# A spectral layer and a rational MoE on one core: the first block's load in two parts, the opening stage reordered

## The chip, the cores and the metric

One core of one Trainium2 chip. The metric is the device time of one execution in microseconds (us); lower is better.

## The reference, cut to what matters

```python
X = np.fft.rfft(x, axis=1)                       # x: 4 x 3008 x 256
Yr = Xr @ w_r - Xi @ w_i + b_r
Yi = Xr @ w_i + Xi @ w_r + b_i
Yr = np.sign(Yr) * np.maximum(np.abs(Yr) - 0.01, 0.0)
Yi = np.sign(Yi) * np.maximum(np.abs(Yi) - 0.01, 0.0)
y = np.fft.irfft(Y, n=3008, axis=1)
h = y.reshape(12032, 256) @ w_in                 # 256 x 2048
P = a[0] + a[1] * h + a[2] * h**2 + a[3] * h**3
Q = 1.0 + abs(b[0]) * np.abs(h) + abs(b[1]) * h**2
out = (P / (Q + 1e-6)) @ w_out                   # 2048 x 256
```

The MoE weights `w_in` and `w_out` come as 64-bit floats and are turned into two 32-bit parts (high and low) on the chip.

## The kernel before, in words

The transform of length 3008 = 47 x 64 is done in two stages of matmuls each way. Per batch element b there are 16 tasks `f1_task` (47-point stage; each copies a 96x512 tile `a` out of PSUM and stores it in HBM, `s1`), 12 tasks `f2_task` (64-point stage on tiles read back from `s1`; the result is split into a high and a low part, `x`), 24 halves `m_task` (the complex mix with `w_r`, `w_i`: 24 matmuls for a pair, then the soft threshold, `yt`) and 12 tasks `i1_task` (first inverse stage; copied as `zt` and stored in HBM, `s2`). `i2_task` does the second inverse stage for a block of five columns, on a tile `ct` loaded from `s2` by `load_c`, and splits it into `xsh` and `xsl`. Then come the MoE units: 8 for each of 26 blocks, each with `g1_mm` (12 matmuls into `h`), a chain on ScalarE, GpSimd and VectorE that starts with ScalarE's Abs (`m<-h`, L356), and `g2_mm` (12 matmuls, or 4 in the last blocks).

All instructions are placed by hand (`manual_schedule`, L485): each engine runs its queue in the order in which the Python code issues it, and every transfer of the program goes out from SyncE (SP), also in order; on that queue a transfer waits until the one eight before it has landed. The order around the change is this:

- *Opening* (L486 to L587). Seven filler matmuls (`warm`, on zeros), the loads of batch element 0, its 16 `f1` tasks with eight stores to `s1`, then loads: `f2` (L563), `wt` (L567), two parts of `b_all` read back from `s1` (256 and 512 KB, L569 and L570), `f2` again, the small inputs `sel`, `bsb`, `eye` (L573 to L580). `prepare` (L501) splits `wt` and builds `selr`, `bias` and `minus`. 28 fillers.
- *Turns* (L588 to L621), p = 0 to 14: `f2` task p, mix p-2, inverse p-3 of batch element 0. In between `convert` runs steps of the weight conversion `from_f64` (five steps to a 512 KB raw piece, 16 pieces; two ScalarE reads L465 and L466, VectorE steps, a ScalarE split L481, a VectorE subtraction): HC[p] steps ahead of the mix, HM[p] behind it, at most two pieces at once. `more_raw` loads two pieces a turn. The copies of `zt` are on VectorE (L272), and stores of `zt` wait in `late` until `flush` in the next turn.
- *Last stage* (L622 to L635): the rest of the conversions, `load_c(0)` as one transfer, eight `f1` tasks of batch element 1 (copies on ScalarE, five buffers), `i2` for block 0 in two halves.
- *The main loop* (L650 on): unit i with parts of the transform of the next batch element between its steps.

PSUM: `bank` gives the tags `ft`, `h` (two buffers each) and, while `early` holds, `acc0`/`acc1` for the mix.

```python
copy(i % 2 if b == 0 else 0, at.rearrange("p j d -> p (j d)"), pt[:96])      # L167
copy(b == 0, zt.rearrange("p k d -> p (k d)"), pt.rearrange("p k d -> p (k d)"))  # L272
```

Of the kernel before, what the change touches and what calls it, by code (L numbers as in the profile page):

```python
# [30 lines left out]
WARM = 28  # L31
HC = (0, 0, 3, 3, 3, 3, 3, 3, 3, 3, 3, 3)
HM = (0, 0, 4, 4, 4, 4, 4, 4, 4, 4, 4, 4, 4, 4)
# [62 lines left out]
def spectral_moe(ctx, tc, t, out):  # L96
# [23 lines left out]
    early = [1]  # L120
    s1 = {}
# [28 lines left out]

    a_t = {}

    def f1_task(b, i):
        c, r = divmod(i, 2)
        if i == 0:
            s1[b] = dram.tile([NK, NG, 2, NJ, D], F32, tag="s1", name="s1")
        pt = bank(b, "f1" if r else "")
        nc.tensor.matmul(out=pt[:96], lhsT=f1, rhs=xin[b, c][:, 2 * r:2 * r + 2, :].rearrange("p j d -> p (j d)"),  # L158
                         start=True, stop=True)
        yield  # L160
        if b == 0:
            if not r:
                a_t[0] = const.tile([128, 4, D], F32, tag=f"wsp{c}", name="a")[:96]
            at = a_t[0][:, 2 * r:2 * r + 2]
        else:
            at = (pro if early else sm).tile([128, 2, D], F32, tag="a", name="a", bufs=5 if early else 3)[:96]
        copy(i % 2 if b == 0 else 0, at.rearrange("p j d -> p (j d)"), pt[:96])  # L167
        yield
        if r:
            del xin[b, c]  # L170
            ahead = 4 if b == 1 and c < 4 else 2
            if b and c + ahead < NJ // 4 and not (b == 1 and c in (2, 3)):
                load_x(b, c + ahead)
        if b == 0:
            if r:
                nc.sync.dma_start(out=s1[b].rearrange("k g c j d -> (k g c) j d")[:, 4 * c:4 * c + 4, :], in_=a_t[0])
            return
        o = 4 * c + 2 * r
        nc.sync.dma_start(out=s1[b].rearrange("k g c j d -> (k g c) j d")[:, o:o + 2, :], in_=at)

    late = []

    def flush():
        while late:
            late.pop(0)()
# [77 lines left out]
    def i1_task(b, p):  # L263
        if p == 0:
            s2[b] = dram.tile([NK, NG, 2, NJ, D], F32, tag="s2", name="s2")
        yt = y_t.pop((b, p))
        pt = bank(b, "i1").rearrange("p (k d) -> p k d", k=2)
        for k in range(2):
            nc.tensor.matmul(out=pt[:, k, :], lhsT=g1[:, 2 * p + k, :], rhs=yt[:, k, :], start=True, stop=True)  # L269
        yield  # L270
        zt = sm.tile([128, 2, D], F32, tag="a", name="zt", bufs=3)
        copy(b == 0, zt.rearrange("p k d -> p (k d)"), pt.rearrange("p k d -> p (k d)"))  # L272
        yield
        dst = s2[b][2 * p:2 * p + 2].rearrange("k g c j d -> (g c j) k d")
        late.append(lambda: nc.sync.dma_start(out=dst, in_=zt))
# [3 lines left out]
    c_t = {}  # L279

# [204 lines left out]
    with tc.manual_schedule():  # L485
# [7 lines left out]
        def warm(n):  # L493
            pt = bank(1, "")
            for _ in range(n):
                nc.tensor.matmul(out=pt, lhsT=idle[:, :128], rhs=idle, start=True, stop=True)
# [4 lines left out]
        def prepare():  # L501
            for wt, h, l in zip(wts, ("wrh", "wih"), ("wrl", "wil")):
                nc.scalar.activation(out=wmix[h], in_=wt, func=ACTF.Copy)
                nc.vector.tensor_tensor(out=wmix[l], in0=wt, in1=v32(wmix[h]), op=ALU.subtract)
# [10 lines left out]

        w_in = t["w_in"].rearrange("(c p) f -> p c f", p=128)
# [5 lines left out]
        running = []  # L522

# [9 lines left out]
        def convert(n):  # L533
            while n:
                if len(running) < 2 and len(done) < len(raws) and (not running or running[0][1] >= 2):
# [4 lines left out]
                pick = running.pop(0)  # L540
                pick[1] += 1
                n -= 1
                if pick[1] < STEPS:
                    next(pick[0])
                    running.append(pick)
                else:
                    drain(pick[0])

# [20 lines left out]
        load_all(0, 2)  # L569
        load_all(2, 4)  # L570
        load_f2(4, 12)
        sel = pro.tile([4, 130], F32, tag="sel", name="sel", bufs=1)
        nc.sync.dma_start(out=sel, in_=t["sel"])  # L573
        bsb = pro.tile([4, D], F32, tag="bsb", name="bsb", bufs=1)
        blo = pro.tile([4, D], F32, tag="blo", name="blo", bufs=1)
        for k, nm in enumerate(("b_r", "b_i")):
            nc.sync.dma_start(out=bsb[2 * k:2 * k + 2, :],
                              in_=t[nm].rearrange("(o d) -> o d", o=1).to_broadcast([2, D]))
        eye = pro.tile([128, 128], F32, tag="eye", name="eye", bufs=1)
        nc.sync.dma_start(out=eye, in_=t["minus"])  # L580
        prepare()
# [51 lines left out]
        for _ in range(4):  # L633
            for g in pair:
                next(g, None)  # L635
# [121 lines left out]
```

## Time and profile before

| | |
|---|---|
| median of 3 runs | 1498.63 us (1495.12 to 1498.64) |
| profiled execution: its own time | 1499.35 us |
| its span | 1497.6 us |
| TensorE matmuls, busy | 1472.0 us, 98% of the span |
| VectorE, busy | 1390.6 us, 93% |
| ScalarE, busy | 1279.7 us, 85% |
| GpSimd, busy | 478.2 us, 32% |
| bytes read and written in HBM | 49.96 and 37.49 MB |
| first MoE matmul (`h`, L332) | 118.04 us |

Times are counted from the start of the span. A busy TensorE is not TensorE at its peak, since matmuls overlap; idle time of an engine counts only where another waits for it. "Granted clock" is the share of full speed (2.4 GHz) that the chip gave TensorE.

### The profile page before, as it was taken

How to read it: one execution, taken by the hardware profiler on the slowest of the kernel's cores; microseconds unless marked ns; L12 is line 12 of the kernel's file. 1: busy time of each engine (PE TensorE's matmuls, PEld its weight loads, DVE VectorE, ACT ScalarE, POOL GpSimd, SP SyncE). 2: the span in 40 equal slices, each digit the busy share in tenths (PEclk: the TensorE clock that was granted, in tenths of full speed). 3: DMA queues.
4: the chain of work that ended last, by engine and by line, in shares of the span. 5: the costliest groups of instructions: out<-in, count | busy, mean ns of one | idle time of the engine just before them, and what ended most of it. 6: DMA issues, size and time to landing. Idle time of an engine off the chain costs nothing.

```text
span 1497.6 us, 19703 instructions
## 1 busy us (share of the span) xinstructions
PE 1472.0 (98%) x7342; PEld 1229.0 (82%) x7343; DVE 1390.6 (93%) x1349; ACT 1279.7 (85%) x1517; POOL 478.2 (32%) x230
## 2 busy tenths in 40 slices
PE   8998999999999999999999999999999999999997
PEld 3876999999878999989878999998986777777776
DVE  2765989999999899999999999999999999999998
ACT  2657888889889889898899989898888999999986
POOL 0102222323323222332323343333333343333332
PEclk9999999999999999999999999999999999999999
DMA  8934111111132111110233011101010000000000
GB/s 265 363 96 149 46 45 42 41 55 33 61 115 76 35 42 42 41 56 29 59 106 91 28 35 48 35 27 48 21 48 14 26 14 27 26 13 27 8 14 22
DMA packets 52976, 88.72 MB, mean 59 GB/s; under 512 B 5032, under 2 KB 37104, under 8 KB 52752
## 3 DMA queue, kind: packets, MB, share of 16 engines
q1 hardware_dynamic: 52880, 87.46, 18.5%
q8 instruction: 58, 0.95, 0.3%
q14 instruction: 38, 0.31, 0.1%
HBM read 49.96 MB, written 37.49 MB: 58 GB/s over the span
## 4 chain that ended last, share of the span: by engine, by line
PE 87%; DVE 6%; issue 3%; DMA 2%; ACT 2%; SPq 0%; DVEq 0%; ACTq 0%
PE acc L424 34%; PE h L332 32%; PE pft L251 7%; PE pi L302 4%; PE pft L158 3%; PE pft L211 2%; PE pft L269 2%; PE pm L251 1%; DVE t L371 1%; DVE t L388 1%; DVE p L386 1%; PE pft L233 1%; PE pi L233 1%; DVE t L373 1%; DMA s<-a 1%
## 5 line engine op out<-in xcount | busy, mean ns | idle before, releaser
L360 POOL TENSOR_TENSOR v<-w,m 128x940 f32<-128x940 f32 (+1 forms) x208 | 456.6, 2195 | 919.4 <-DVE p L386 468.3
L332 PE MATMUL h<-xsh,win 128*128 128x470 f32 (+1 forms) x1664 | 451.0, 393 | 2.4 <-DVE t L373 2.4
L424 PE MATMUL acc<-g,wsp 128*128 128x470 f32 (+1 forms) x1908 | 433.2, 375 | 3.2 <-DVE g L391 3.2
L424 PEld LDWEIGHTS acc<-g,wsp 128*128 128x128 f32 x1908 | 357.7, 189 | 53.1 <-DVE g L391 5.5
L332 PEld LDWEIGHTS h<-xsh,win 128*128 128x128 f32 x1664 | 304.9, 190 | 63.5 <-issue 22.2
L373 DVE SCALAR_TENSOR_TENSOR t<-t,small,h 128x940 f32<-128x940 f32 (+1 forms) x208 | 244.9, 1177 | 6.1
L358 ACT ACTIVATE w<-m,small 128x940 f32<-128x940 f32 (+1 forms) x208 | 241.6, 1162 | 6.9
L371 DVE TENSOR_TENSOR t<-t,h 128x940 f32<-128x940 f32 (+1 forms) x208 | 231.2, 1111 | 12.1 <-ACT t L359 11.8
L332 PE MATMUL h<-xsl,win 128*128 128x470 f32 (+1 forms) x832 | 242.4, 372 | 0.0
L365 ACT ACTIVATE y<-v 128x940 f32<-128x940 f32 (+1 forms) x207 | 202.1, 976 | 39.5 <-DVE g L391 32.6
L359 ACT ACTIVATE t<-h,small 128x940 f32<-128x940 f32 (+1 forms) x208 | 229.8, 1105 | 0.0
L366 ACT ACTIVATE y<-y 128x940 f32<-128x940 f32 (+1 forms) x207 | 203.1, 981 | 6.6
L356 ACT ACTIVATE m<-h 128x940 f32<-128x940 f32 (+1 forms) x208 | 194.2, 934 | 12.7 <-PE h L332 9.8
L391 DVE TENSOR_TENSOR g<-t,y 128x940 fp32r<-128x940 f32 (+1 forms) x158 | 178.3, 1129 | 23.2 <-PE acc L424 22.1
L383 DVE SCALAR_TENSOR_TENSOR g<-t,small,y 128x940 fp32r<-128x940 f32 (+1 forms) x158 | 192.8, 1220 | 1.6 <-ACT y L366 1.6
L388 DVE SCALAR_TENSOR_TENSOR t<-t,small,p 128x940 f32<-128x940 f32 (+1 forms) x159 | 189.9, 1195 | 0.0
L386 DVE SCALAR_TENSOR_TENSOR p<-v,g 128x940 f32<-128x940 f32 (+1 forms) x159 | 178.7, 1124 | 0.2
L332 PEld LDWEIGHTS h<-xsl,win 128*128 128x128 f32 x832 | 155.5, 188 | 20.6
L424 PE MATMUL acc<-g,f 128*128 128x470 f32 (+1 forms) x392 | 156.7, 541 | 1.6 <-DVE g L400 1.6
L424 PEld LDWEIGHTS acc<-g,f 128*128 128x128 f32 x392 | 73.6, 189 | 59.9 <-issue 54.2
L251 PE MATMUL pft<-wrh,x 128*128 128x256 f32 x288 | 75.2, 283 | 0.0
L251 PE MATMUL pft<-wih,x 128*128 128x256 f32 x288 | 75.1, 283 | 0.0
(94 smaller groups left out, 1446.8 us busy)
## 6 DMA issues: line engine op xcount, KB each, us to landing
xin<-in_x SPq DMA_DIRECT2D x32, 384.0 KB, 4.1
s<-zt SPq DMA_DIRECT2D x48, 256.0 KB, 2.2
out_t<-ob SPq DMA_DIRECT2D x50, 235.0 KB, 2.2
ct<-s SPq DMA_DIRECT2D x22, 480.0 KB, 4.3
s<-a SPq DMA_DIRECT2D x48, 192.0 KB, 2.9
bt<-s SPq DMA_DIRECT2D x36, 256.0 KB, 2.9
raw_win<-in_w_in SPq DMA_DIRECT2D x8, 512.0 KB, 8.6
raw_wsp<-in_w_out SPq DMA_DIRECT2D x8, 512.0 KB, 8.1
```

Of the source, the lines that this page charges most:

```text
L251: nc.tensor.matmul(out=pt[:, k, :], lhsT=l, rhs=r, start=False, stop=n == len(ops) - 1, skip_group_check=True)
L332: nc.tensor.matmul(out=h[:, i, :w], lhsT=l, rhs=r, start=k == 0, stop=k == len(ops) - 1)
L356: nc.scalar.activation(out=d["m"], in_=h, func=ACTF.Abs)
L358: nc.scalar.activation(out=d["w"], in_=d["m"], func=ACTF.Identity, scale=cb[:, 1:2], bias=cb[:, 0:1])
L359: nc.scalar.activation(out=d["t"], in_=h, func=ACTF.Identity, scale=a[:, 3:4], bias=a[:, 2:3])
L360: nc.gpsimd.tensor_tensor(out=d["v"], in0=d["w"], in1=d["m"], op=ALU.mult)
L365: nc.scalar.activation(out=d["y"], in_=d["v"], func=ACTF.Square, bias=C0)
L366: nc.scalar.activation(out=d["y"], in_=d["y"], func=ACTF.Abs_reciprocal_sqrt)
L371: nc.vector.tensor_tensor(out=tt, in0=tt, in1=h, op=ALU.mult)
L373: nc.vector.scalar_tensor_tensor(out=tt, in0=tt, scalar=d["a"][:, 1:2], in1=h, op0=ALU.add, op1=ALU.mult)
L388: stt(out=tt, in0=tt, scalar=a0, in1=p, op0=ALU.add, op1=ALU.subtract)
L424: nc.tensor.matmul(out=acc[n][e][:, :w], lhsT=l[:, e * 128:(e + 1) * 128], rhs=r, start=begun[n] == 1 and k == 0, stop=begun[n] == UB and ...
```

## The change

Parts that belong together: (1) the first block's `ct` is loaded by `load_first_c` in two transfers, the rows of the first 22 frequencies as soon as their stores are out, the last 8 rows after the last store; (2) six instead of eight `f1` tasks of batch element 1 run before `i2`, with six buffers, their copies in turn on ScalarE and VectorE, their stores held in `late`; two more run between the two `i2` steps, on the `h` banks; (3) the small inputs are loaded before the first stores and prepared in the 14th `f1` task, the weights `wt` come after the first part of `b_all`, whose second load is split in two, and `f2`'s first load goes into the `f1` loop; (4) conversions: eight steps a turn (four and four), up to three pieces at once, all done in turn p = 11; (5) `zt` copies are on ScalarE but for p = 10; (6) five fillers after each of the first two `f2` tasks, and 26 instead of 28 ahead.

```diff
-WARM = 28
-HC = (0, 0, 3, 3, 3, 3, 3, 3, 3, 3, 3, 3)
-HM = (0, 0, 4, 4, 4, 4, 4, 4, 4, 4, 4, 4, 4, 4)
+WARM = 26
+FILL = 6
+HC = (0, 0, 4, 4, 4, 4, 4, 4, 4, 4, 4, 4)
+HM = (0, 0, 4, 4, 4, 4, 4, 4, 4, 4, 4, 4, 0, 0)
...
-        pt = bank(b, "f1" if r else "")
+        pt = bank(b, "f1" if r or closed else "")
...
-            at = (pro if early else sm).tile([128, 2, D], F32, tag="a", name="a", bufs=5 if early else 3)[:96]
-        copy(i % 2 if b == 0 else 0, at.rearrange("p j d -> p (j d)"), pt[:96])
+            fill = early and not closed
+            at = (pro if fill else sm).tile([128, 2, D], F32, tag="a", name="a", bufs=FILL if fill else 3)[:96]
+        copy(i % 2 if early else 0, at.rearrange("p j d -> p (j d)"), pt[:96])
...
-        nc.sync.dma_start(out=s1[b].rearrange("k g c j d -> (k g c) j d")[:, o:o + 2, :], in_=at)
+        send = lambda: nc.sync.dma_start(out=s1[b].rearrange("k g c j d -> (k g c) j d")[:, o:o + 2, :], in_=at)
+        late.append(send) if early else send()
...
-        copy(b == 0, zt.rearrange("p k d -> p (k d)"), pt.rearrange("p k d -> p (k d)"))
+        copy(b == 0 and p == NK // 2 - 2, zt.rearrange("p k d -> p (k d)"), pt.rearrange("p k d -> p (k d)"))
...
+    def load_first_c(k):
+        if not first_c:
+            first_c.append(sm.tile([96, JB, D], F32, tag="c", name="ct", bufs=1))
+        r = slice(0, 4 * k) if k < NK else slice(4 * (NK - 2), 4 * NK)
+        nc.sync.dma_start(out=first_c[0][r], in_=s2[0].rearrange("k g c j d -> (k g c) j d")[r, :JB, :])
+        c_t[0] = first_c[0]
...
         def convert(n):
             while n:
-                if len(running) < 2 and len(done) < len(raws) and (not running or running[0][1] >= 2):
+                if len(running) < 3 and len(done) < len(raws) and (not running or running[-1][1] >= 2):
                     running.append([from_f64(*raws[len(done)]), 0])
                     done.append(1)
                 if not running:
                     return
-                pick = running.pop(0)
+                turn[0] += 1
+                pick = running[turn[0] % len(running)]
...
+        load_small()
         for i in range(16):
             drain(f1_task(0, i))
-        load_f2(0, 4)
+            if i == 9:
+                load_f2(0, 4)
+            if i == 13:
+                prepare_small()
         wts = []
+        load_all(0, 2)
         for nm in ("w_r", "w_i"):
...
-        load_all(0, 2)
-        load_all(2, 4)
+        load_all(2, 2)
+        load_all(4, 2)
         load_f2(4, 12)
...
+            if p < 2:
+                warm(5, "m")
             flush()
+            if p == np_ + 2:
+                load_first_c(NK - 2)
...
         flush()
-        while running or len(done) < len(jobs):
-            convert(1)
-        load_c(0)
-        for _ in range(8):
+        assert not running and len(done) == len(jobs)
+        load_first_c(NK)
+        for _ in range(FILL):
             drain(first.pop(0)[3])
-        early.clear()
+        closed.append(1)
         pro_stack.close()
...
         pair = [i2_task(0, ec) for ec in range(2)]
-        for _ in range(4):
-            for g in pair:
-                next(g, None)
+        rest_f1 = [first.pop(0)[3] for _ in range(2)]
+        for g in pair + rest_f1 + pair + pair + pair:
+            next(g, None)
+        for g in rest_f1:
+            drain(g)
+        early.clear()
```

`load_small` and `prepare_small` hold the lines on `sel`, `bsb`, `eye` that stood after the `f1` loop and in `prepare`.

The order of instructions at three places follows; line numbers of the changed kernel are some 4 to 30 higher than those of the kernel before, and the numbers behind names tell buffers apart.

ScalarE in turn p = 4, before (`raw_win4` is the fifth raw piece, `yt` the mix's threshold, L465 and L466 the two reads, L481 the split):

```order
L216 ACTIVATE x_412<-pft_407 128x4x128
L481 ACTIVATE win2_420<-e_355 128x2x256
L257 ACTIVATE yt_450<-pm_424 128x512
L465 ACTIVATE e_454<-raw_win4_276 128x512
L466 ACTIVATE r_455<-raw_win4_276 128x512
```

and in the changed kernel:

```order
L220 ACTIVATE x_425<-pft_420 128x4x128
L478 ACTIVATE e_432<-raw_win4_287 128x512
L479 ACTIVATE r_433<-raw_win4_287 128x512
L494 ACTIVATE win2_437<-e_351 128x2x256
L494 ACTIVATE win3_440<-e_404 128x2x256
L261 ACTIVATE yt_469<-pm_443 128x512
```

The fifth raw piece is now read ahead of the third `yt`, with two splits between them.

VectorE at the end of the turns, before (L476, L468, L470, L483 are conversion steps):

```order
L147 COPY zt_942<-pft_939 128x512
L260 SCALAR_TENSOR_TENSOR yt_971<-pm_945,yt_971 128x512
L476 ISA e_887<-e_887,r_888 128x1024
L468 TENSOR_SCALAR e_935<-e_935 128x512
L483 TENSOR_TENSOR wsp6_975<-e_887,wsp6_975 128x2x256
L470 SCALAR_TENSOR_TENSOR e_935<-raw_wsp7_541,e_935 128x512
L147 COPY zt_983<-pft_980 128x512
L147 COPY zt_989<-pft_986 128x512
```

and in the changed kernel:

```order
L496 TENSOR_TENSOR wsp7_919<-e_878,wsp7_919 128x2x256
L264 SCALAR_TENSOR_TENSOR yt_957<-pm_931,yt_957 128x512
L264 SCALAR_TENSOR_TENSOR yt_992<-pm_966,yt_992 128x512
L149 COPY zt_998<-pft_995 128x512
L149 COPY a_1017<-pft_1015 96x512
```

The conversions lie ahead of the last two `yt`, one `zt` copy is left, and the copies of the `f1` tasks follow.

SyncE behind the turns in the changed kernel (`s2<-zt` are stores of the inverse, `s1<-a` those of the `f1` tasks):

```order
L279 DMA s2_414<-zt_963 128x2x256
L279 DMA s2_414<-zt_998 128x2x256
L291 DMA ct_1001<-s2_414 88x1280
L279 DMA s2_414<-zt_1006 128x2x256
L291 DMA ct_1001<-s2_414 8x1280
L144 DMA xin_1019<-in_x 96x1024
```

The first part of `ct` stands between the last two stores, the second part behind the last.

## Rows read from the trace of the kernel before

**Rows 1.** Windows: TensorE, its weight loads, VectorE, ScalarE, GpSimd; clock, DMA share, GB/s
```profile
200.00:300.00 100.00, 100.00 (x556) 90.71 (x555) 94.08 (x89) 87.94 (x104) 31.29 (x14) 1.00 0.13 41
```
**Rows 2.** Timeline of TensorE, the opening: start us, us, instruction, idle before it
```profile
22.57 6.21 PE L496 MATMUL pft<-idle 128*128 128x512 bf16 x27
30.68 1.13 PE L211 MATMUL pft<-f,b_all 128*128 128x128 f32 x8 [1.90 <-DMA b_all<-s]
33.64 3.76 PE L211 MATMUL pft<-f,b_all 128*128 128x128 f32 x16 [1.83 <-DMA b_all<-s]
37.75 0.80 PE L244 MATMUL pm<-bias,selr 128*128 128x512 f32 x1 [0.35 <-DVE bias L514]
...
43.41 0.40 PE L233 MATMUL pft<-x,minus 128*128 128x512 f32 x1
```
**Rows 3.** Windows, the opening
```profile
34.00:36.00 2.00, 2.00 (x11) 2.00 (x11) 0.49 (x2) 0.21 (x1) 0.00 (x0) 0.50 1.06 366
```
**Rows 4.** Timeline of SyncE's queue: the fifth and sixth raw piece
```profile
41.86 3.33 SPq L530 DMA_DIRECT2D raw_win<-in_w_in x2
```
**Rows 5.** DMA issues in 41.8 to 43.5 us: count, KB each, us to landing
```profile
raw_win<-in_w_in SPq DMA_DIRECT2D x2, 512.0 KB, 12.8
```
**Rows 6.** Timeline of ScalarE: conversion of the fifth raw piece
```profile
54.50 0.66 ACT L465 ACTIVATE e<-raw_win 128x512 f32<-128x512 f32 x1
...
56.86 0.63 ACT L481 ACTIVATE win<-e 128x512 fp32r<-128x512 f32 x1 [1.14 <-DVE e L476]
```
**Rows 7.** Timeline of TensorE, the turns: starts of mixes, and one stall
```profile
60.52 0.48 PE L244 MATMUL pm<-bias,selr 128*128 128x512 f32 x1
...
70.56 0.50 PE L233 MATMUL pft<-x,minus 128*128 128x512 f32 x1 [1.59 <-ACT x L216]
...
82.74 0.47 PE L244 MATMUL pm<-bias,selr 128*128 128x512 f32 x1
...
87.83 0.47 PE L244 MATMUL pm<-bias,selr 128*128 128x512 f32 x1
...
92.17 0.58 PE L244 MATMUL pm<-bias,selr 128*128 128x512 f32 x1
...
97.23 0.59 PE L244 MATMUL pm<-bias,selr 128*128 128x512 f32 x1
```
**Rows 8.** Windows, sum of 60 to 100 us in pieces of 2 us
```profile
sum 40.00, PE 37.59 PEld 35.59 DVE 32.81 ACT 27.51 POOL 5.84; mean PE 1.88 PEld 1.78 DVE 1.64 ACT 1.38 POOL 0.29
```
**Rows 9.** Timeline of VectorE: the copies of the last two inverse tiles
```profile
104.61 1.28 DVE L147 COPY zt<-pft 128x512 f32<-128x512 f32 x2
```
**Rows 10.** Timeline of TensorE, the last stage
```profile
102.09 1.13 PE L269 MATMUL pft<-yt,g 128*128 128x256 f32 x4 [0.55 <-DVE yt L260]
...
105.34 6.25 PE L158 MATMUL pft<-xin,small 96*96 96x512 f32 x14 [1.26 <-DVE zt L147]
113.35 1.32 PE L302 MATMUL pi<-small,ct 96*128 96x94 f32 x10 [1.76 <-DMA ct<-s]
115.89 2.45 PE L302 MATMUL pi<-small,ct 96*128 96x94 f32 x10 [1.21 <-ACT a L149]
118.04 2.10 PE L332 MATMUL h<-xsh,win 128*128 128x470 f32 x4
```
**Rows 11.** Chain that ended last, in the main loop: twelve MoE matmuls
```profile
160.51 2.59 PE h L332 x12
```
**Rows 12.** DMA issues in 102 to 109 us, then in the first 160 us
```profile
s<-zt SPq DMA_DIRECT2D x2, 256.0 KB, 2.2
ct<-s SPq DMA_DIRECT2D x1, 480.0 KB, 4.8
...
bt<-s SPq DMA_DIRECT2D x3, 256.0 KB, 2.8
```
**Rows 13.** Timeline of ScalarE: the first MoE Abs
```profile
122.63 0.95 ACT L356 ACTIVATE m<-h 128x940 f32<-128x940 f32 x1 [3.69 <-PE h L332]
```
**Rows 14.** Windows, the last stage
```profile
116.00:118.00 2.00, 2.00 (x10) 2.00 (x11) 0.65 (x1) 0.82 (x2) 0.00 (x0) 0.50 1.01 370
```

More of the change, by code (lines that the diff above doesn't have):

```diff
@@ L120, in spectral_moe @@
     early = [1]
+    closed = []
     s1 = {}
@@ L149, in copy, with flush @@
             nc.scalar.activation(out=out, in_=in_, func=ACTF.Copy)
+    late = []
+    def flush():
+        while late:
+            late.pop(0)()
     a_t = {}
@@ L178, in f1_task @@
         o = 4 * c + 2 * r
-        nc.sync.dma_start(out=s1[b].rearrange("k g c j d -> (k g c) j d")[:, o:o + 2, :], in_=at)
[L181 to L185, printed above, removed]
+        send = lambda: nc.sync.dma_start(out=s1[b].rearrange("k g c j d -> (k g c) j d")[:, o:o + 2, :], in_=at)
+        late.append(send) if early else send()
     b_t = {}
@@ L279, in spectral_moe @@
     c_t = {}
+    first_c = []
+    def load_first_c(k):
[4 more added lines that the diff above has]
+        c_t[0] = first_c[0]
     def load_c(n):
@@ L491, in spectral_moe, with warm @@
         nc.vector.memset(idle, 0.0)
-        def warm(n):
-            pt = bank(1, "")
+        def warm(n, kind=""):
+            pt = bank(1, kind)
             for _ in range(n):
@@ L500, in spectral_moe, with load_small, prepare_small @@
             load_x(0, c)
[L501 to L504, printed above, removed]
+        sel = pro.tile([4, 130], F32, tag="sel", name="sel", bufs=1)
+        bsb = pro.tile([4, D], F32, tag="bsb", name="bsb", bufs=1)
+        blo = pro.tile([4, D], F32, tag="blo", name="blo", bufs=1)
+        eye = pro.tile([128, 128], F32, tag="eye", name="eye", bufs=1)
+        def load_small():
+            nc.sync.dma_start(out=sel, in_=t["sel"])
+            for k, nm in enumerate(("b_r", "b_i")):
+                nc.sync.dma_start(out=bsb[2 * k:2 * k + 2, :],
+                                  in_=t[nm].rearrange("(o d) -> o d", o=1).to_broadcast([2, D]))
+            nc.sync.dma_start(out=eye, in_=t["minus"])
+        def prepare_small():
             nc.vector.memset(v32(selr), 0.0)
@@ L514, in prepare, with prepare_mix @@
                 nc.vector.scalar_tensor_tensor(out=bias[:4, k], in0=blo, scalar=sel[:, 129:130], in1=bsb, op0=ALU.mult, op1=ALU.add)
+        def prepare_mix():
+            for wt, h, l in zip(wts, ("wrh", "wih"), ("wrl", "wil")):
+                nc.scalar.activation(out=wmix[h], in_=wt, func=ACTF.Copy)
+                nc.vector.tensor_tensor(out=wmix[l], in0=wt, in1=v32(wmix[h]), op=ALU.subtract)
         w_in = t["w_in"].rearrange("(c p) f -> p c f", p=128)
@@ L522, in spectral_moe @@
         running = []
+        turn = [0]
         def more_raw(n):
@@ L544, in convert @@
                     next(pick[0])
-                    running.append(pick)
                 else:
                     drain(pick[0])
+                    running.remove(pick)
         done = []
@@ L568, in spectral_moe @@
             wts.append(wt)
-        load_all(0, 2)
-        load_all(2, 4)
+        load_all(2, 2)
+        load_all(4, 2)
         load_f2(4, 12)
[L572 to L581, printed above, removed]
+        prepare_mix()
         np_ = NK // 2
```

## The prediction, made before the changed kernel was run

> **What bounds the kernel now.** I read the windows first, then the timeline of each engine over the first 125 us, then the transfers. From 200 us on TensorE is busy all the time at the full clock: the window shows 100.00 us of work in 100 us [rows 1]. The change leaves the order of that stretch as it is, on every engine, so it can only move its start. What counts is one moment: when ScalarE takes the first MoE unit, its Abs at 122.63 us [rows 13]. Everything behind it follows in the same order, and a microsecond won there should be a microsecond of the end.
>
> Before that moment there are three stages. In the start, the first second-stage matmuls (L211) wait 1.90 and 1.83 us for the intermediate that comes back from HBM, and the bias matmul waits 0.35 us for VectorE [rows 2]. The granted clock falls to 0.50 of full there, the 1.2 GHz level [rows 3], after those idle pieces, and the first mix runs from 37.75 to 43.41 us. In the middle, turns of one f2 pair, one mix and one inverse follow each other; 82.74 to 87.83 us is a turn with no stall, 5.09 us [rows 7]. In the last stage VectorE copies the last two inverse tiles only at 104.61 us [rows 9], in a queue where weight conversions stand ahead of them; TensorE waits for `ct` until 113.35, then 1.21 us more for a ScalarE copy of a first-stage task, and the first MoE matmul comes at 118.04 [rows 10], at half clock [rows 14].
>
> **The start: nothing kept.** `b_all` is fetched as 256 KB, two weights, 256 KB, 256 KB. The second part is smaller than the 512 KB that ended the wait at 33.64 us, so I put the first mix at about 35.3 us instead of 37.75, and at full clock it is some 2.5 us shorter, as the fillers stand in the idle pieces. Ten fillers cost 2.3 us (27 took 6.21 us, 0.23 each [rows 2]), two fewer at the front give 0.5 back. The small inputs go to the queue before the first stores; that takes away the 0.35 us. Their VectorE and ScalarE steps go between the last two first-stage copies, where both engines wait for TensorE. So the second turn could end 5 us sooner.
>
> But ScalarE is a queue in order, and it reads raw weights. The fifth raw transfer is issued at 41.86 us [rows 4] and that pair lands after 12.8 us [rows 5], so about 54.3; ScalarE takes it at 54.50 [rows 6], behind the third `yt`. With four steps per half turn the fifth raw comes before the third `yt`. The bytes ahead of it are the same to within 0.5 MB, and the transfers were running all the time, so I let it land between 52.5 and 54.3 us. Behind it on ScalarE stand its second read, two weight splits, the `yt`, the sixth raw's two reads, an `x`, a `zt` and the next turn's `x`: ten steps of 0.5 to 0.66 us [rows 6], 5.7 us together. Only then can TensorE finish that turn; with 1.8 us of inverse and f2 matmuls the fifth mix starts between 60.0 and 61.8 us, against 60.52 now [rows 7]. **Term 1 is 0**, bounds -1.3 (later) and +2 (if the transfers run without gaps and land 2 us sooner still). If this cover of raw transfers were not there the start would be worth the 5 us.
>
> **The middle.** From the fifth to the twelfth mix it is 60.52 to 97.23, 36.71 us. Five turns of 5.09, one of 4.34 (87.83 to 92.17, no f2 left in it) and one of 4.1 (that one less the correction matmul) are 33.9, so 2.8 us are stalls, 1.59 of them one wait for ScalarE, before 70.56 [rows 7]. Up to three conversions in flight, and `zt` copies moved from VectorE, loosen this coupling. But ScalarE gets more: it is busy 27.51 us of 40 [rows 8], and eight `zt` copies of 0.6 add 4.8, conversions at 8 steps a turn for 7 another 2.9 or so; that is 35 of 40, 88%. It still fits in a turn. **Term 2 is 2.0 us gained**, bounds 0 (new stalls of the same size) and 2.8.
>
> **The last stage.** Let E be the end of the last inverse matmuls, now 102.09+1.13=103.22, which is 5.99 us after the start of the twelfth mix; that stays. Now: the Abs comes at E+19.4. After the change, step by step. VectorE holds no conversions here, so it copies the last but one `zt` about 0.5 us before E, and ScalarE the last at E+0.65 (now E+2.7). The store of the first of these two lands 2.2 us after issue [rows 12], and part A of `ct` (88 rows) goes out at E+2.0. The last store stands behind that on the same queue: issued at E+2.35, landed near E+4.9, for part A runs beside it. Part B (8 rows) goes at E+5.0. No row shows so small a load on a free queue; the nearest are 2.2 for a 256 KB store and 2.8 for a 256 KB load [rows 12], so 2.0 to 3.5, and I take 2.4: `ct` is there at E+7.4 (now E+10.1). Six first-stage tasks at 0.87 us (14 half-records took 6.25 [rows 10]) end at E+5.2, their copies on two engines with a buffer each, so none waits for a store. TensorE idles 2.2 us. Then two `i2` groups, 2.3 us together (one took 1.32 to its last result [rows 10]), so E+9.7, the two first-stage tasks (E+11.4), in whose shadow `xsh` and `xsl` are made, and the first MoE matmuls, 2.6 us at full clock for twelve [rows 11] (now 4.6 from the first matmul to the Abs [rows 10, 13]): Abs at E+14.05. **Term 3 is 5.35 us gained.** Bounds: 3.9 (part B lands 1.5 later) and 6.4 (stores land faster).
>
> Splitting `ct` itself gives little: with one load behind both stores it would come at E+0.65+2.2+4.8=E+7.65 by [rows 12].
>
> **Sum.** 0+2.0+5.35=7.4 us. The profiled execution took 1499.35 us, 0.7 above the median of the runs, 1498.63. Its time becomes 1492.0, and the median 1491.3; I say 1491. Bounds added up: gains of 2.6 to 11.2.
>
> **Rivals.** *The clock falls again.* TensorE idles 2.2 us before `i2`; now it idles 1.76 and 1.21 with 1.3 of work between, and the clock is at 0.50 behind that [rows 10, 14]. For it: the total idle is not much less. Against it: six tasks without a gap stand ahead. It would run an `i2` group more slowly (+1.1, 2.45 against 1.32 [rows 10]), two tasks (+1.7) and the first MoE matmuls (+1.7), so 4.5 of the gain go: 1495.8. The Trainium skill, page "TensorE: Matmul & The Clock Gate", Part 1, says that the gate halves the clock after idle time and that its look at the engine runs free of the program, so the same program can fall on either side; by that this rival may come in some executions only. The rows agree that idle pieces precede the fall. *The store chain does not shorten*: the last store, held behind part A on the queue, lands as late as `ct` is served now, and the middle keeps its stalls: about 3 us are left, 1495.6. *ScalarE becomes the bound, slower.* Raw weights are asked for a turn earlier, and each wait in front of a raw or for a VectorE step holds `x`, `yt` and now `zt` too, in a queue that is 88% full. If each of ten turns lost 1.59 us as the one at 70.56 did, 15.9 go, less 7.4: 1507. It decides from 0.75 us a turn. Against it: ScalarE waited that long once in eight turns [rows 7], and the two engines share less now. *It does not do what it says*: that all conversions are done by turn twelve can be read from the order of instructions, so I give this nothing.
>
> **How the numbers follow.** The sum as worked out 0.65, clock rival 0.17, chain rival 0.10, ScalarE rival 0.08. The first one's own range is 1487 to 1495. About 0.3% (4.5 us) is what a measurement of this kernel tells from no change. Nearly all of the first case (gains over 4.5) is faster, 0.62 of its 0.65; the clock and chain rivals, with the other terms at their better bounds, give another 0.08: faster 0.70. Slower is the ScalarE rival, 0.07, and the rest, 0.23, is the same. The range takes in the two middle rivals up to 1496.5, and at the low side gains of 12 us.
>
> **What would show it.** Right: `ct` part B issued 5 us after the last inverse matmul, the first MoE Abs near 115, no granted clock of 0.5 after 35 us, the fifth raw read before the third `yt` with ScalarE idle before it. Wrong for term 1: the fifth mix well before 58 us. Wrong altogether: an Abs later than 120, or idle time of TensorE behind it that is not there now.

## The result, and the profile after

The changed kernel takes 1513.22 us (median of 4 runs, 1510.67 to 1514.13), beside 1497.5 us (1495.12 to 1498.64) for the kernel before in the same comparison: ratio 1.0104, interval 1.0085 to 1.0124. It is 1% slower, and lies outside the predicted range. The profiled execution took 1512.64 us, with a span of 1510.9 us.

The windows of the changed kernel (TensorE, weight loads, VectorE, ScalarE, GpSimd; granted clock, DMA share, GB/s), for the turns, the last stage and the main loop:

```profile
60.00:100.00 40.00, 34.41 (x247) 31.93 (x246) 29.20 (x52) 31.28 (x60) 5.67 (x7) 1.00 0.56 184
...
120.00:122.00 2.00, 0.00 (x0) 0.00 (x0) 0.00 (x0) 0.00 (x0) 0.00 (x0) 0.85 0.31 61
122.00:124.00 2.00, 1.68 (x8) 1.71 (x9) 0.00 (x0) 0.00 (x0) 0.00 (x0) 0.50 0.97 295
...
200.00:300.00 100.00, 100.00 (x553) 90.55 (x552) 92.70 (x88) 87.60 (x106) 31.26 (x14) 1.00 0.13 42
```

The main loop is as full as before [rows 1]. In the turns TensorE lost 3.18 us of work in 40 (34.41 against 37.59 [rows 8]), and in the last stage it stands still and then runs at half clock. Where each piece went is in its timeline (start us, us, instruction, idle before it):

```profile
31.25 1.13 PE L215 MATMUL pft<-f,b_all 128*128 128x128 f32 x8 [2.96 <-DMA b_all<-s]
...
39.97 0.47 PE L248 MATMUL pm<-bias,selr 128*128 128x512 f32 x1
...
44.19 0.48 PE L248 MATMUL pm<-bias,selr 128*128 128x512 f32 x1
...
49.78 0.80 PE L237 MATMUL pft<-x,minus 128*128 128x512 f32 x1 [2.24 <-ACT x L220]
...
53.41 0.48 PE L248 MATMUL pm<-bias,selr 128*128 128x512 f32 x1
...
63.99 0.50 PE L237 MATMUL pft<-x,minus 128*128 128x512 f32 x1 [2.13 <-ACT x L220]
...
65.99 0.48 PE L248 MATMUL pm<-bias,selr 128*128 128x512 f32 x1
...
106.76 0.58 PE L248 MATMUL pm<-bias,selr 128*128 128x512 f32 x1
...
111.62 1.13 PE L273 MATMUL pft<-yt,g 128*128 128x256 f32 x4 [0.55 <-DVE yt L264]
...
122.32 4.55 PE L315 MATMUL pi<-small,ct 96*128 96x94 f32 x20 [4.42 <-DMA ct<-s]
126.66 3.62 PE L166 MATMUL pft<-xin,small 96*96 96x512 f32 x4
131.92 1.93 PE L345 MATMUL h<-xsh,win 128*128 128x470 f32 x4 [1.63 <-ACT a L151]
```

The first mix comes at 39.97 us (37.75 [rows 2]), the fifth at 65.99 and the twelfth at 106.76 (60.52 and 97.23 [rows 7]). The last inverse matmuls end at 111.62+1.13 = 112.75, called E as in the prediction; before, E was 103.22. ScalarE of the changed kernel:

```profile
47.55 0.66 ACT L478 ACTIVATE e<-raw_win 128x512 f32<-128x512 f32 x1 [1.21 <-DMA raw_win<-in_w_in]
...
49.15 0.58 ACT L220 ACTIVATE x<-pft 128x512 fp32r<-128x512 f32 x1
...
57.07 0.67 ACT L478 ACTIVATE e<-raw_win 128x512 f32<-128x512 f32 x1 [2.72 <-DMA raw_win<-in_w_in]
...
61.24 0.68 ACT L478 ACTIVATE e<-raw_win 128x512 f32<-128x512 f32 x1 [1.41 <-issue]
...
130.37 1.01 ACT L318 ACTIVATE xsh<-pi 128x470 fp32r<-128x470 f32 x2 [12.70 <-PE pft L166]
...
136.26 0.95 ACT L369 ACTIVATE m<-h 128x940 f32<-128x940 f32 x1 [4.39 <-issue]
```

The first MoE Abs starts at 136.26 us, 13.63 later than at 122.63 [rows 13]. From it to the end of the span it is 1374.64 us, and 1374.97 before: all of the loss lies ahead of this instruction. Counted between the same events, by these rows and those of before, it falls into four pieces:

| us | before | after | loss |
|---|---|---|---|
| second fillers to the first mix | 15.18 | 17.45 | 2.27 |
| first to fifth mix | 22.77 | 26.02 | 3.25 |
| fifth to twelfth mix | 36.71 | 40.77 | 4.06 |
| E to the Abs | 19.41 | 23.51 | 4.10 |

The second fillers (L496, now L509) are those behind the first stage; they start when the first-stage matmuls are done, at 22.57 us before [rows 2] and 22.52 after.

The first two pieces are better read together. Before, the second and the third mix start here:

```profile
44.46 0.47 PE L244 MATMUL pm<-bias,selr 128*128 128x512 f32 x1
...
49.54 0.47 PE L244 MATMUL pm<-bias,selr 128*128 128x512 f32 x1
```

In the changed kernel the second starts at 44.19 us, 0.27 sooner: its first mix starts later but runs at full clock (1.00 from 40 to 44 us), where before it ran at half (0.50 from 38 to 42 us). So the 5.5 us lost up to the fifth mix all lie behind the second: 4.1 between the second and the third, where TensorE waits for an `x` that stands behind a raw read on ScalarE (47.55 and 49.15 us) and is at half clock after that (0.50 from 50 to 52 us), and 1.6 between the fourth and the fifth, ahead of which ScalarE waits 2.72 us for the fifth raw piece. Ahead of that piece the transfers had run with gaps. The windows of 24 to 30 us, before and after:

```profile
24.00:30.00 6.00, 4.72 (x22) 1.94 (x20) 0.83 (x2) 1.26 (x2) 0.00 (x0) 1.00 0.84 263
```
```profile
24.00:30.00 6.00, 4.24 (x19) 1.75 (x18) 1.01 (x3) 0.00 (x0) 0.00 (x0) 1.00 0.33 90
```

The DMA share fell from 0.84 to 0.33. Before, `f2`'s first load and the two weights went out at 23.88 to 25.11 us, ahead of `b_all`; after, `f2` goes out at 18.67 and the weights behind `b_all`, at 28.70 and 29.21.

What ScalarE and VectorE waited for in the turns is in the waits of the changed kernel, 60 to 108 us (engine, line, waited for: us, times, longest):

```profile
ACT wsp L494 <- DVE e L489: 7.0, 5, 2.6
...
PE pft L237 <- ACT x L220: 5.6, 6, 2.1
...
ACT e L478 <- issue: 3.1, 2, 1.7
```

From 38 to 125 us TensorE waits 7.8 us in seven pieces for ScalarE's `x` (L220), where before it was 2.1 us in two. And SyncE's queue of the changed kernel, the first `b_all`, the fifth raw pair and the last stage:

```profile
28.26 0.38 SPq L582 DMA_DIRECT2D b_all<-s  x1
...
44.36 3.53 SPq L558 DMA_DIRECT2D raw_win<-in_w_in  x2
...
114.49 0.31 SPq L291 DMA_DIRECT2D ct<-s  x1
114.85 0.36 SPq L279 DMA_DIRECT2D s<-zt  x1
120.12 0.29 SPq L291 DMA_DIRECT2D ct<-s  x1
```

Part A of `ct` goes out at E+1.74, the last store at E+2.10, a little ahead of the forecast E+2.0 and E+2.35. But the store takes 5.3 us to land instead of 2.2 [rows 12], by the DMA issues in 113 to 125 us:

```profile
ct<-s SPq DMA_DIRECT2D x1, 440.0 KB
s<-zt SPq DMA_DIRECT2D x1, 256.0 KB, 5.3
```

### The profile page after: what moved, and what is told of

The parts are those of the page before. It is cut to its first block, busy times and chain, and to the rows that moved or that the text cites. A ratio compares the mean times of both kernels' runs of the same rounds, so it can differ in the third digit from the quotient of the medians.

```text
span 1510.9 us, 19719 instructions
## 1 busy us (share of the span) xinstructions
PE 1477.0 (98%) x7350; PEld 1230.4 (81%) x7351; DVE 1384.6 (92%) x1342; ACT 1283.5 (85%) x1524; POOL 477.8 (32%) x230
## 4 chain that ended last, share of the span: by engine, by line
PE 85%; DVE 3%; ACT 2%; issue 2%; DMA 0%; DVEq 0%; ACTq 0%
PE acc L437 34%; PE h L345 32%; PE pft L255 7%; PE pi L315 4%; PE pft L215 2%; PE pft L273 2%; PE pft L166 2%; PE pi L237 1%; PE pft L248 1%; PE pft L237 1%; DVE t L384 1%; DVE t L401 0%; ACT t L372 0%; ACT m L369 0%; DVE t L386 0%
## 5 line engine op out<-in xcount | busy, mean ns | idle before, releaser
L315 PEld LDWEIGHTS pi<-small,ct 96*128 96x128 f32 x512 | 67.0, 197 | 10.4 <-issue 8.1
```

## The experiments

Edits are to the changed kernel. Four theories stood against each other: the order of the conversions, the `zt` copies on ScalarE, the transfers of `ct`, and the place of the two `f1` tasks between the `i2` steps.

**x1: the conversions as before.**

```diff
-HC = (0, 0, 4, 4, ...
-HM = (0, 0, 4, 4, ...
+HC = (0, 0, 3, 3, ...
+HM = (0, 0, 4, 4, 4, 4, 4, 4, 4, 4, 4, 4, 4, 4)
...
-                if len(running) < 3 and len(done) < len(raws) and (not running or running[-1][1] >= 2):
+                if len(running) < 2 and len(done) < len(raws) and (not running or running[0][1] >= 2):
...
-        assert not running and len(done) == len(jobs)
+        while running or len(done) < len(jobs):
+            convert(1)
```

> The changed kernel with the old conversion schedule alone (7 steps a turn, two pieces at once, the rest behind the turns). In the changed kernel the fifth mix starts at 65.99, the twelfth at 106.76, the first MoE Abs comes at 136.26 us. Theory 'queues' (eight steps a turn, three pieces at once hold ScalarE up): the fifth mix starts 3 to 5 us sooner, the twelfth at 100 to 102, the Abs near 131. Rival 'start' (the raw weights land later, because the loads behind the first stage go out later): fifth mix stays at 64 to 66, twelfth above 104, Abs above 134. Rival 'zt' (the copies moved to ScalarE): the same as 'start' here.

1506.56 us, ratio 1.0072 (1.0057 to 1.0087). The fifth to the twelfth mix is 36.13 us again, and the first to the fifth 23.50. Its windows and waits, 60 to 100 and 60 to 108 us:

```profile
60.00:100.00 40.00, 38.02 (x278) 35.95 (x276) 27.56 (x47) 30.95 (x59) 7.43 (x7) 1.00 0.50 168
...
ACT wsp L494 <- DVE e L489: 8.3, 6, 2.1
```

ScalarE is about as busy as in the changed kernel (30.95 against 31.28 us of 40), and still waits 8.3 us for VectorE, but TensorE has its 38.02 us of work. So the loss in the turns is not the amount of ScalarE's work: it is what stands in its queue ahead of `x` when it waits. The `zt` copies are on ScalarE here too, and cost nothing beside the old conversions. The last stage got longer, 26.46 us from E to the Abs: the trailing conversions hold the last but one `zt` copy on VectorE until 103.18, 1.4 us behind E, with both transfers of `ct` behind it.

**x2: `zt` copies on VectorE.**

```diff
-        copy(b == 0 and p == NK // 2 - 2, zt...
+        copy(b == 0, zt...
```

> The changed kernel with all copies of inverse tiles on VectorE again. Theory 'zt' (these copies fill ScalarE's queue): the seven waits of TensorE for ScalarE's x in the turns, 7.8 us in the changed kernel, fall below 3, the twelfth mix starts near 102 instead of 106.76. Theories 'queues' and 'start': the twelfth mix moves by under 1.5 us.

1509.30 us, 1.0090 (1.0075 to 1.0105). Fifth to twelfth mix 38.67 us, against 40.77: some 2 us of the loss in the turns are the copies, by single profiles, and only beside the changed conversions (x1). From 38 to 125 us TensorE still waits 6.2 us in five pieces for ScalarE's `x`, 4.1 of them in one piece before 60 us; the forecast of under 3 was missed. The intervals of the two totals overlap.

**x3: `ct` in one load behind both stores.**

```diff
-            if p == np_ + 2:
-                load_first_c(NK - 2)
...
-        load_first_c(NK)
+        load_c(0)
```

> The changed kernel with the first block loaded at once behind both stores. Theory 'store behind part A' (the last store goes out 2.6 us late and needs 5.3 us because 440 KB are under way beside it): ct is there about 2.5 us sooner after the last inverse matmul than the 9.6 us of the changed kernel, TensorE idles 2 us instead of 4.4, the total falls by 2 to 3 us, by 5 if the clock then stays up. Rival (splitting helps as meant): the total rises by 2 or more.

1508.92 us, 1.0090 (1.0073 to 1.0106). TensorE and the DMA issues of this kernel, last stage:

```profile
118.89 3.03 PE L315 MATMUL pi<-small,ct 96*128 96x94 f32 x20 [2.40 <-DMA ct<-s]
```
```profile
s<-zt SPq DMA_DIRECT2D x4, 256.0 KB, 2.1
...
ct<-s SPq DMA_DIRECT2D x1, 480.0 KB, 4.4
```

E is 111.35 here, so `i2` starts at E+7.54, where the split load gave E+9.57. So the split costs two microseconds instead of saving some. E to the Abs: 20.28 us. By the totals this is less sure: 1.0104 and 1.0090, with intervals that overlap.

**x4: the last two `f1` tasks ahead of `i2`.**

```diff
         closed.append(1)
+        for _ in range(2):
+            drain(first.pop(0)[3])
         pro_stack.close()
...
-        rest_f1 = [first.pop(0)[3] for _ in range(2)]
+        rest_f1 = []
```

> The changed kernel with the last two first-stage tasks ahead of the i2 pair again instead of behind it. Theory 'memory reuse' (xsh lies where the tile of the last two tasks lay, so ScalarE's first xsh waits for these tasks: it starts at 130.37 though its matmuls ended near 124.6): xsh comes 4 to 5 us sooner, the Abs 3.5 to 5 us sooner, total 3.5 to 5 lower. Rival (xsh waits for something else, or the loads set the pace): total within 1 us.

1506.93 us, 1.0073 (1.0058 to 1.0088). ScalarE of this kernel:

```profile
122.35 0.56 ACT L318 ACTIVATE xsh<-pi 128x470 fp32r<-128x470 f32 x1 [4.70 <-PE pi L315]
```

`xsh` now waits for its own matmuls (which start at 120.34), not for those of the `f1` tasks as at 130.37 above, and E to the Abs is 17.78 us, 5.7 less. Not all of this is the wait of `xsh`: 3.62 us are the matmuls of the two tasks themselves, which here run while TensorE would wait for `ct` (its idle piece shrinks from 4.42 to 2.35 us), and 1.63 are the idle piece ahead of the first MoE matmul at 131.92, which waited for a copy of these tasks that stands behind `xsh` on ScalarE. The pool `mx`, in which `xsh` lies, is opened after the pools of the opening are closed, over the memory of the input tile that these two tasks still read; with the tasks between the `i2` steps, writing `xsh` has to wait until they have run. The run shows the wait and that it goes with the tasks' place; that memory is the link is read from the code.

**x5: two pieces at once, eight steps a turn.** As x1, with HC and HM left as changed; the order in which steps of several pieces take turns is the old one too.

```diff
-                if len(running) < 3 and len(done) < len(raws) and (not running or running[-1][1] >= 2):
+                if len(running) < 2 and len(done) < len(raws) and (not running or running[0][1] >= 2):
```

> The changed kernel, still eight conversion steps a turn, but with two pieces at once in the old rotation. It parts the two halves of the conversion change. From the fifth to the twelfth mix the changed kernel takes 40.8 us, with the old conversions as a whole 36.1. Theory 'too many steps' (eight steps a turn fill the queues): 39 to 41 us here. Rival 'three pieces' (a third piece waits for its e and r tiles and holds ScalarE): 36 to 38 us here.

1509.70 us, 1.0085 (1.0072 to 1.0098). Fifth to twelfth mix 39.26 us, between x1 (36.13) and the changed kernel (40.77): the eight steps make the larger part, the third piece with its order of steps some 1.5 us, by single profiles.

**y1: only the last stage changed.** The opening, the conversions and the turns' `zt` copies as before (the last two `zt` on ScalarE), one `ct` load, the eight `f1` tasks ahead of `i2`.

```diff
-        copy(b == 0 and p == NK // 2 - 2, zt...
+        copy(b == 0 and p < NK // 2 - 2, zt...
```

> The opening, the conversions and the copies of the kernel before, and of the change only the last stage, mended: the last two zt copies on ScalarE, the first block in one load, eight first-stage tasks ahead of i2 with copies on two engines and late stores. Theory: the last inverse matmul ends near 103 us as before, ct is there 8 us later, nothing waits in front of xsh, the Abs comes 14 to 16 us after the last inverse matmul instead of 19.4: 117 to 119 us, total 3.5 to 5.5 us below the kernel before. Rival (the clock is low behind the idle piece and eats it): total within 2 us of before.

1490.12 us (5 runs, 1489.43 to 1492.19), 0.9959 (0.9947 to 0.9971): faster than both kernels. E to the Abs is 14.08 us, where the kernel before has 19.41.

**y2: y1 with the changed opening.** Against y1:

```diff
+        load_small()
         for i in range(16):
             drain(f1_task(0, i))
+            if i == 9:
+                load_f2(0, 4)
+            if i == 13:
+                prepare_small()
...
```

> The same as the kernel with the last stage only, and the changed opening (small inputs first, second fetch in two parts, fillers between). Theory 'the opening is hidden by the raw weights': total within 1.5 us of that kernel. Rival 'the opening helps': first mix 2 us sooner and the twelfth too, total 1.5 to 4 us below it. Rival 'the opening harms' (the stores and raw weights go out later): total 1.5 to 4 us above it.

1494.23 us (12 runs, 1490.56 to 1498.22), 0.9984 (0.9974 to 0.9994). This is 4.1 us above y1 by the medians, with intervals apart: the changed opening harms, as the second rival had it. The last stage is instruction for instruction that of y1, yet E to the Abs was 16.87 us in the profile. TensorE and the windows of y2, then of y1:

```profile
112.22 3.88 PE L315 MATMUL pi<-small,ct 96*128 96x94 f32 x20 [1.19 <-DMA ct<-s]
...
114.00:116.00 2.00, 2.00 (x11) 2.00 (x11) 0.65 (x1) 0.56 (x1) 0.00 (x0) 0.50 1.05 404
```
```profile
109.50 2.44 PE L315 MATMUL pi<-small,ct 96*128 96x94 f32 x20 [1.18 <-DMA ct<-s]
...
112.00:114.00 2.00, 1.81 (x8) 1.16 (x7) 0.80 (x2) 0.54 (x1) 0.00 (x0) 1.00 1.06 406
```

After the same idle piece (1.19 and 1.18 us) the granted clock is 0.50 in one, the 1.2 GHz level, and 1.00 in the other. The Trainium skill, page "TensorE: Matmul & The Clock Gate", Part 1, says that the gate's look at the engine runs free of the program; these two rows agree with it. The profiled execution of y2 took 1496.80 us, the second longest of its twelve; no profile shows what the clock did in the others.

**y3: y2 with the first 80 rows of `ct` loaded ahead of the last two stores.** 16 rows follow.

```diff
-            flush()
             if p == np_ + 2:
-                load_first_c(NK - 2)
+                load_first_c(NK - 4)
+            flush()
...
-        r = slice(0, 4 * k) if k < NK else slice(4 * (NK - 2), 4 * NK)
+        r = slice(0, 4 * k) if k < NK else slice(4 * (NK - 4), 4 * NK)
```

> As the kernel with the changed opening and the mended last stage, and the first block in two parts again, but split elsewhere: 80 rows, which need only the stores of earlier turns, go out ahead of the last two stores, and 16 rows behind them. Theory 'what is wrong with the split is its place in the queue': ct is there 5.5 to 6.5 us after the last inverse matmul, before the eighth first-stage task ends, TensorE does not idle and the clock stays up: the Abs 12.5 to 14 us after the last inverse matmul, total 2 to 4 us below the kernel with one load. Rival (the small load is slow beside the stores): ct at 7.5 us or later, total as with one load.

1492.42 us (6 runs, 1491.43 to 1492.83), 0.9969 (0.9958 to 0.9981). TensorE no longer waits for `ct`, and E to the Abs is 12.80 us, as forecast. The total is 1.8 us below y2's, a little less than forecast, and the intervals overlap.

**z1: y1 with that load.** In place of y1's `load_c(0)`:

```diff
+            if p == np_ + 2:
+                load_first_c(NK - 4)
             flush()
...
-        load_c(0)
+        load_first_c(NK)
```

> The opening, the conversions and the copies of the kernel before, the mended last stage, and the first block in two parts with 80 rows ahead of the last two stores. If the parts add up: the twelfth mix starts at 95 to 97.5 us, the Abs comes 12.8 us after the last inverse matmul (14.1 with one load and the clock up, 16.9 with the clock down), so it is at 114 to 116.5, the total 1488.5 to 1490, 6 to 8 us below the kernel before. Rival (the early part disturbs the last turns, since its 400 KB run beside the last stores): total as with one load, 1490 to 1492.

1491.38 us (5 runs, 1489.37 to 1492.20), 0.9962 (0.9949 to 0.9974). SyncE, then the DMA issues in 99 to 108 us and TensorE, of this kernel:

```profile
100.96 0.32 SPq L291 DMA_DIRECT2D ct<-s  x1
102.28 0.87 SPq L279 DMA_DIRECT2D s<-zt  x2
106.03 0.32 SPq L291 DMA_DIRECT2D ct<-s  x1
```
```profile
s<-zt SPq DMA_DIRECT2D x3, 256.0 KB, 3.1
...
ct<-s SPq DMA_DIRECT2D x1, 400.0 KB, 3.7
...
ct<-s SPq DMA_DIRECT2D x1, 80.0 KB, 2.2
```
```profile
101.47 7.45 PE L166 MATMUL pft<-xin,small 96*96 96x512 f32 x16
108.75 2.37 PE L315 MATMUL pi<-small,ct 96*128 96x94 f32 x20
```

The large part goes out ahead of the last two stores and lands at about 104.7, the rest at 108.2, and the eight `f1` tasks reach 108.75: no idle piece, and `i2` at full clock (2.37 us). E to the Abs is 12.96 us, 1.1 less than in y1, but the totals of y1 and z1 cannot be told apart. The twelfth mix (95.64) and the Abs (114.59) came as forecast; the total did not (1488.5 to 1490 was expected).

**z2: the changed kernel with the old opening.**

```diff
-WARM = 26
+WARM = 28
...
-        load_small()
         for i in range(16):
             drain(f1_task(0, i))
-            if i == 9:
-                load_f2(0, 4)
-            if i == 13:
-                prepare_small()
+        load_f2(0, 4)
...
-            if p < 2:
-                warm(5, "m")
```

> The changed kernel with the opening of the kernel before. Theory 'the opening costs' (the steps on the small inputs hold the last first-stage copy up by 1.6 us on VectorE, and the raw weights go out 1.1 us later against the first fetch): total 2 to 4 us below the changed kernel (1509 to 1511). Rival 'hidden': within 1.5 us of it. Rival 'the opening helps, as meant': above it.

1509.18 us (4 runs, 1508.37 to 1510.26), 1.0082 (1.0069 to 1.0096): against 1.0104, the opening costs about 3 us here, with intervals that overlap.

**z3: y3 with the small inputs prepared behind all 16 first-stage tasks.** 

```diff
-            if i == 13:
-                prepare_small()
...
+        prepare_small()
         prepare_mix()
```

> The kernel with the changed opening, old conversions and 80 rows early, but the steps on the small inputs behind all first-stage copies. Theory 'VectorE steps ahead of the last copy': the last copy starts within 0.2 us of the end of its matmul instead of 1.6 us later, the first fetch goes out 1.4 us sooner, the total falls by 1 to 2 us against 1492.4. Rival (the raw weights set the pace anyway, by the transfers ahead of them): under 0.7 us.

1491.26 us (5 runs, 1490.73 to 1491.72), 0.9963 (0.9950 to 0.9975). VectorE of the changed kernel, the end of the first stage:

```profile
21.00 0.69 DVE L149 COPY a<-pft 96x512 f32<-96x512 f32 x1 [1.03 <-PE pft L166]
21.66 0.17 DVE L527 MEMSET selr<- 128x128 f32 x1
...
24.34 0.67 DVE L149 COPY a<-pft 96x512 f32<-96x512 f32 x1
```

and of z3:

```profile
21.34 0.69 DVE L149 COPY a<-pft 96x512 f32<-96x512 f32 x1 [1.03 <-PE pft L166]
```

The last matmul of that stage ended at 22.68 us in the changed kernel and at 21.31 in z3; the copy came 1.66 us behind it in the changed kernel, at once in z3. The last store and the first `b_all` stand behind that copy: `b_all` goes out 4.59 us after the start of the fillers in z3 and 5.74 in the changed kernel and in y3. The first mix did not come sooner for it (16.12 us after the fillers, 15.33 in y3), the fifth did, by 0.75 us. The total is 1.2 us below y3's, within the intervals.

**z4: the changed kernel, only its last stage mended** (the 80 rows early as in y3, the eight `f1` tasks ahead of `i2` as in x4).

```diff
-            flush()
             if p == np_ + 2:
-                load_first_c(NK - 2)
+                load_first_c(NK - 4)
+            flush()
...
+        for _ in range(2):
+            drain(first.pop(0)[3])
         pro_stack.close()
```

> The changed kernel with its own opening, conversions and copies, and only the last stage mended (80 rows early, eight first-stage tasks ahead of i2). It measures what the last stage alone costs in the change. Theory: the twelfth mix stays at 103 to 107 us, the Abs comes 12.8 to 14 us after the last inverse matmul instead of 23.5, total 9 to 11 us below the changed kernel, near 1503. Rival (part of the late stage comes from the turns, so mending it frees less): total above 1506.

1501.56 us (5 runs, 1501.09 to 1502.26), 1.0034 (1.0021 to 1.0047). E to the Abs is 12.42 us, fifth to twelfth mix 41.58.

All kernels by their profiles, in us (second fillers to first mix, first to fifth, fifth to twelfth, E to the Abs):

| | opening | to 5th | to 12th | last |
|---|---|---|---|---|
| before | 15.18 | 22.77 | 36.71 | 19.41 |
| changed | 17.45 | 26.02 | 40.77 | 23.51 |
| x1 | 17.27 | 23.50 | 36.13 | 26.46 |
| x2 | 15.68 | 27.34 | 38.67 | 23.90 |
| x3 | 15.88 | 27.91 | 41.08 | 20.28 |
| x4 | 15.47 | 28.14 | 40.76 | 17.78 |
| x5 | 15.56 | 26.73 | 39.26 | 24.25 |
| y1 | 14.29 | 22.47 | 36.79 | 14.08 |
| y2 | 15.46 | 23.69 | 36.71 | 16.87 |
| y3 | 15.33 | 25.08 | 35.18 | 12.80 |
| z1 | 13.52 | 24.32 | 35.31 | 12.96 |
| z2 | 14.08 | 27.32 | 40.75 | 23.75 |
| z3 | 16.12 | 23.54 | 35.10 | 12.67 |
| z4 | 15.70 | 28.52 | 41.58 | 12.42 |

The table leaves out the piece from the twelfth mix to E: 5.98 to 6.00 us, but 7.29, 7.50, 7.08 and 6.76 in x3, x4, z2 and z4.

The first two columns should be added up. The changed kernel, x3, x4 and z4 have the same instructions up to the fifth mix; their first columns differ by 2.0 us, the sums of the two only by 0.75. From the fillers to the fifth mix it is 36.76 to 37.95 us with the old opening and the old conversions (before, y1, z1), 39.15 to 40.77 with the changed opening (x1, y2, y3, z3), 41.40 with the changed conversions and the old opening (z2), and 43.47 to 44.22 with both (changed, x3, x4, z4). So the opening costs about 2.4 us there with either conversions, and the conversions about 3.8 with either opening, by single profiles. The loss by the opening goes with the fifth raw pair: SyncE issues it 19.1 to 19.5 us after the start of the fillers in the four kernels with the old opening, and 20.5 to 22.6 in the ten others.

The seven kernels with the old conversions (before, x1, y1 to y3, z1, z3) take 23.6 and 36.0 us in the turns, the five with the changed ones and the changed `zt` copies 27.6 and 41.0: 9 us together.

The ratios say the same: from the changed kernel to z4 0.0070 (the last stage as it was changed, against a mended one), from z4 to y3 0.0065 (conversions and `zt`), from y3 to z1 0.0007 (opening; the intervals overlap), and z1 is 0.0038 below the kernel before. Of 1497 us that is 10.5, 9.7, 1.0 and a gain of 5.7; 10.5+9.7+1.0-5.7 = 15.5 is the loss. For the opening other pairs give more: 0.0025 from y1 to y2 and 0.0022 from z2 to the changed kernel, 3.7 and 3.3 us.

## Why the prediction was wrong, point by point

**What counts.** Right: everything is decided by the first Abs, and the rest is a shift (1374.64 and 1374.97 us behind it).

**Term 1, the start (0; bounds -1.3 and +2).** Wrong by 5.5 us at the fifth mix. The step that failed: "The bytes ahead of it are the same to within 0.5 MB, and the transfers were running all the time, so I let it land between 52.5 and 54.3 us." They were not running all the time: the DMA share from 24 to 30 us is 0.33, not 0.84. The queue reached the fifth raw at 44.36, not 41.86 [rows 4], and ScalarE took it at 57.07, 12.7 us behind its issue as before. That is 2.77 us behind the latest time allowed, and another wait of ScalarE behind it, 1.41 us at 61.24, was put at nothing; together they are the 4.2 us by which the fifth mix (65.99) misses 61.8. That ScalarE would meet the wait for this transfer was seen; that it would also be issued later was not.

The first mix was wrong too, expected 2.4 us sooner and 2.2 later. "Their VectorE and ScalarE steps go between the last two first-stage copies, where both engines wait for TensorE": VectorE's idle piece there is about one microsecond (1.03 at 21.00), and the steps from 21.66 to 24.34 take 2.7. So `b_all` goes out 5.74 us after the start of the fillers, where before it was 4.32, and its smaller second part is no help: TensorE has it 6.61 us behind that issue, before 6.75. The five fillers behind it took 2.34 us at half clock (0.50 from 36 to 38 us), twice what was put down. But that first mix ran at full clock, "some 2.5 us shorter", and with that, which was right, the second mix was not late at all.

**Term 2, the middle (2.0 gained).** Wrong: 4.06 us lost. The step that failed is "loosen this coupling", with "It still fits in a turn": both take a share of busy time for what an in-order queue can hide. The share came out near 78% (31.28 of 40), below the forecast 88%, and TensorE lost time all the same. Four steps in a row, and a third piece between them, put two splits and two reads ahead of an `x`; each split waits for VectorE's L489, and a read can find no free `e` buffer (the 1.41 us at 61.24 have no releaser in the profile; the buffer is argued from the three that the pool has, and from VectorE's step L496, which reads an `e` and ends at 61.16). x1 with nearly the same busy share has none of this loss. The *ScalarE rival*, given 0.08, is what happened, with about 0.6 us in each of seven turns by the profile, under the 0.75 that was named, and the last stage did the rest.

**Term 3, the last stage (5.35 gained).** Wrong: 4.10 us lost, in three steps. "The last store ... landed near E+4.9, for part A runs beside it": it landed near E+7.4, since beside 440 KB of part A it took 5.3 us (2.1 in x3, where no load runs beside it). This is near to the *store chain rival*, which was given 0.10, but the store was not held up on the queue: it went out on time and landed late. `ct` came 2.17 us later than forecast. Next, "the two first-stage tasks, in whose shadow `xsh` and `xsl` are made": `xsh` waited for these tasks, by the code since it lies in memory that they read, and TensorE then stood still for 1.63 us ahead of the first MoE matmul. The prediction went by names of tiles alone, and took no account of where they lie. Third, the idle piece of 4.42 us, and the *clock rival* (0.17) on top, which cost the most: the granted clock is 0.50 from 122 us, and `i2`, the two tasks and the first MoE matmuls take 4.34, 3.62 and 4.34 us where 2.3, 1.7 and 2.6 were put down, 5.7 us together. About 1.1 of that is not the clock: at full clock z1 takes 3.69 us from its first MoE matmul to the Abs. What was right: "Splitting `ct` itself gives little: with one load behind both stores it would come at E+7.65" (x3: E+7.54), the issue times of part A and the last store, and that this stage holds the gain: y1, with one load and all eight tasks ahead, reaches E+14.08 and 0.9959, z1 E+12.96.

**The chances.** The three rivals were taken one at a time, and all three came together, wholly or in part. They are not independent: the late store made `ct` late, and the clock fell behind the idle piece that this left.

**Open.** How the loss in the turns divides between the eight steps, the third piece and the `zt` copies is known only from single profiles (x2, x5). The opening costs 1.0 us by the totals of z1 and y3, and over 3 by the pairs y1 and y2, z2 and the changed kernel; up to the fifth mix it is 2.4 by the profiles. No run puts the weights alone back ahead of `b_all`, or leaves out the five fillers. That `xsh` waits for memory is read from the code; no run moves it to other memory.

## What to carry to other kernels

Before moving work to an engine with free time, write down what will stand in its queue ahead of the instruction that the bottleneck waits for, and what each of these waits for itself; a busy share says nothing on that (31.28 and 30.95 us of 40 here, with 7.8 and 2.7 us of waits from 38 to 125 us). When loads are put in another order, look at what is left to run while the queue waits for a store: here the DMA share fell from 0.84 to 0.33, and a load far behind came 2.5 us later. A split load took away TensorE's wait where its large part went out ahead of the last stores (y3, z1), and cost time where a store that others wait for runs beside it (x3). When a buffer is opened over memory just released, look who still reads that memory: work placed "in the shadow" can be what the buffer waits for (x4).

## What the runs showed that was not expected

The start differs from one execution to the next, with the same instructions. The first-stage copies on ScalarE come at 7.35, 10.76, 13.27 and 14.99 us in the changed kernel, and at 6.22, 7.93, 9.65 and 11.37 in x1, and the stage ends at 22.5 and 18.9 us. TensorE's rows look like two speeds (four matmuls in these 2 us against six), but the clock column reads 1.00 in both. The windows of the changed kernel and of x1:

```profile
8.00:10.00 2.00, 2.00 (x4) 0.81 (x3) 0.69 (x1) 0.00 (x0) 0.00 (x0) 1.00 1.03 279
```
```profile
8.00:10.00 2.00, 2.00 (x6) 0.77 (x5) 0.69 (x1) 0.88 (x2) 0.00 (x0) 1.00 1.02 260
```

The cause was not settled. It is why stages are counted here from event to event, and totals by medians.
